# An attention and MLP kernel on one core: hand-placed order against a list scheduler, with new loads, hash moves and relus

## The chip, the cores and the metric

The kernel runs on one core of a Trainium2 chip. The metric is device time in microseconds (us), as the median of several executions. Before the change it was 365.38 us (3 runs, 363.77 to 365.77). TensorE does matmuls, VectorE and ScalarE work on elements, GpSimd also works on elements, and SyncE ("sync") mostly issues DMAs. The profiles count the DMA queues of all issuing engines on the same 16 DMA engines. "PSUM" is the memory that matmuls write to.

A run is called slow when it is over 1.5% above the fastest run of the same kernel.

## The reference

```python
# q, k, v: (4, 8, 768, 64); proj: (64, 6); w_ch1: (512, 2048); w_ch2: (2048, 512)
q_bits = (np.einsum('bhsd,dk->bhsk', q, proj) > 0)
k_bits = (np.einsum('bhsd,dk->bhsk', k, proj) > 0)
mask = q_bucket[:, :, :, None] == k_bucket[:, :, None, :]   # all six bits equal
scores = np.where(mask, scale * np.matmul(q, k.transpose(0, 1, 3, 2)), -1e9)
attn = softmax(scores)                     # (shortened here)
x = np.matmul(attn, v)                     # heads side by side: (4, 768, 512)
xn = (x - mu) / np.sqrt(var + 1e-06) * g_ln
out = x + np.maximum(xn @ w_ch1, 0.0) @ w_ch2
```

The mask is computed as more score: a matmul over the six hash bits adds a large value for each equal bit, and a bias in the exp takes the total away again.

## The kernel before

The work is 72 steps (batch, 256 queries, 4 heads, 256 keys): scores on TensorE, exp on ScalarE, and attention times v ("av") on TensorE. Every six steps finish a unit of 256 tokens. A unit is normalized on VectorE and turned by two transposing DMAs into the tile `xnT`. Then come 8 chunks of ff1 with a relu each, and 8 chunks of ff2. Chunks of unit u are placed between the steps of later units. Each function has a key, and the keys, set by hand, decide the order.

```python
def load_x(b, g, t):                       # q or k of the next batch, a whole tile
    nc.sync.dma_start(out=X[b, g, t], in_=qk_view((q, k)[t], b, g))
def hash_move(b, g, c, i):                 # 16 for each group: bits of 6 partitions to their place
    nc.sync.dma_start(out=G[b, g][32*i : 32*i+NB, :, W*c : W*c+W],
                      in_=Bt[b, g][32*c + 8*i : 32*c + 8*i + NB])
def flip(u):
    for qt in range(2):
        nc.sync.dma_start_transpose(out=xnT[u][:, qt], in_=xc[u][:, qt])
def ff1(u, p, bank):
    ...                                    # 8 matmuls that read xnT[u]
    nc.vector.tensor_scalar_max(hb[u][:, 2*p : 2*p+2], f1, 0.0)
...
at(S0 - 10, load_x, b, g, 0)               # S0: the first step that needs the group
at(6 * u + 6.12, flip, u)
```

Loads, moves, transposes and stores go through one queue, sync's; only w2 (GpSimd) and small constants (ScalarE) take another.

The softmax here doesn't subtract the row's maximum and nothing guards it: scores larger than these inputs give would overflow.

## Time and profile before

| | before |
|---|---|
| span of the profiled run | 363.9 us |
| TensorE busy | 312.7 us (86%) |
| first ff1 starts | 65.0 us |
| from there to the end | 298.9 us |
| ff1 waits for relus / for `xnT` | 13.8 / 2.3 us |

The chain of waits shows what a transposed tile takes from issue to landing (start, duration, what):

```profile
113.38 2.44 DMA xnT<-xc
189.57 2.50 DMA xnT<-xc
266.80 2.43 DMA xnT<-xc
```

### The profile page before, as it was taken

What the parts mean: (1) busy time and instruction counts of PE and PEld (TensorE: products, weight loads), DVE (VectorE), ACT (ScalarE), POOL (GpSimd) and SP (SyncE); (2) the same over time, 40 slices, a digit from 0 to 9 for tenths busy, and PEclk for the clock granted to TensorE, in tenths of its full rate; (3) what the DMA queues carried; (4) which work ended last, traced back from release to release, by engine and by line L of the source; (5) the groups of instructions that cost most, each with busy time, mean ns of one, the idle gap of its engine ahead of it and who ended that gap; (6) DMA issues with size and microseconds to landing.
All of it is one profiled execution on the core that took longest, in us unless ns stands there. A gap on an engine that the chain in (4) does not pass through costs nothing.

```text
span 363.9 us, 9678 instructions
## 1 busy us (share of the span) xinstructions
PE 312.7 (86%) x4281; PEld 209.8 (58%) x4344; DVE 183.3 (50%) x373; ACT 144.7 (40%) x76; POOL 100.5 (28%) x106
## 2 busy tenths in 40 slices
PE   8674457989988989989989989898889899897993
PEld 3353335766665666756656657666656567565561
DVE  1427245385662363578444534955624545446341
ACT  2344204662453554445246445533535455442000
POOL 1656142019940010069710010399200100101000
PEclk9989555899999999999999999999999999999899
DMA  7799931991021039860030279700210302203022
GB/s 170 174 243 212 306 112 29 273 260 23 9 64 34 3 88 278 193 141 7 12 78 13 59 204 242 192 7 8 64 35 2 88 2 59 31 2 78 10 59 58
DMA packets 34873, 35.68 MB, mean 98 GB/s; under 512 B 17424, under 2 KB 29712, under 8 KB 34832
## 3 DMA queue, kind: packets, MB, share of 16 engines
q1 hardware_dynamic: 31872, 32.96, 36.0%
q0 software_dynamic: 2112, 2.10, 3.6%
q8 instruction: 34, 0.56, 0.6%
q10 hardware_dynamic: 848, 0.01, 0.2%
q14 instruction: 7, 0.06, 0.1%
HBM read 27.27 MB, written 6.29 MB: 92 GB/s over the span
## 4 chain that ended last, share of the span: by engine, by line
PE 66%; DVE 15%; SPq 5%; DMA 4%; issue 3%; ACT 3%; POOL 1%; ACTq 0%; DVEq 0%; POOLq 0%
PE f L248 19%; PE f L258 18%; PE sc L182 11%; PE acc L206 8%; PE hf L301 4%; SPq L133 4%; DVE hb L252 3%; ACT E L189 3%; PE hp L123 2%; DVE xc L231 2%; DMA w1f<-in_moe_w_ch_dram 2%; DMA xnT<-xc 2%; PE warm L354 2%; DVE x L221 2%; DVE st L223 1%
## 5 line engine op out<-in xcount | busy, mean ns | idle before, releaser
L189 ACT ACTIVATE E<-sc,bias_sb 128x2048 bf16<-128x2048 f32 x72 | 141.6, 1967 | 173.9 <-PE sc L182 173.9
L248 PE MATMUL f<-xnT,w_sb 128*128 128x256 bf16 x768 | 99.7, 274 | 16.3 <-DVE hb L252 13.8
L248 PEld LDWEIGHTS <-w_sb 128*128 128x128 bf16 x768 | 72.4, 98 | 39.1 <-issue 23.0
L252 DVE TENSOR_SCALAR hb<-f 128x512 bf16<-128x512 f32 x96 | 65.6, 683 | 52.7 <-PE f L248 51.4
L258 PE MATMUL f<-w_sb,hb 128*128 128x512 bf16 x321 | 86.9, 385 | 3.5
L232 POOL TENSOR_SCALAR rs<-mv 128x2 f32<-128x2 f32 x12 | 6.1, 512 | 199.6 <-DVE mv L230 199.6
L182 PE MATMUL sc<-qb,kb 32*128 32x256 bf16 x1152 | 54.2, 275 | 0.0
L258 PEld LDWEIGHTS <-hb 128*128 128x128 bf16 x384 | 35.2, 99 | 30.5 <-issue 3.2
L206 PEld LDWEIGHTS <-E 128*128 128x128 bf16 x1152 | 43.1, 100 | 11.4 <-issue 10.5
L206 PE MATMUL acc<-vaug,E 128*128 128x65 bf16 x1152 | 49.5, 198 | 0.0
L265 DVE SCALAR_TENSOR_TENSOR res<-f,rs,x 128x512 f32<-128x512 f32 x24 | 18.0, 751 | 54.7 <-PE f L258 50.7
L182 PE MATMUL sc<-G 6*128 6x256 bf16 x576 | 41.9, 280 | 4.0 <-ACT E L189 3.9
L97 POOL TENSOR_SCALAR qb<-T 128x1536 bf16<-128x1536 f32 (+1 forms) x10 | 30.6, 3059 | 13.4 <-DVE T L288 13.4
L182 PEld LDWEIGHTS <-G 6*128 6x128 bf16 x576 | 15.4, 92 | 29.7 <-issue 28.6
L182 PEld LDWEIGHTS <-kb 32*128 32x128 bf16 x1152 | 30.8, 96 | 2.0
L301 PE MATMUL hf<-T,pfull 128*128 128x256 f32 x48 | 18.1, 514 | 13.6 <-DVE T L288 13.5
L83 DVE STREAM_TRANSPOSE T<-X 128x384 f32<-128x384 f32 x48 | 25.4, 555 | 0.0
L301 PEld LDWEIGHTS hf<-T,pfull 128*128 128x128 f32 x48 | 10.7, 246 | 18.7 <-DVE T L288 17.2
L223 DVE BATCH_NORM_STATS2 st<-x 128x6 f32<-128x256 f32 x48 | 18.1, 418 | 0.8
L221 DVE TENSOR_TENSOR x<-acc,rc 128x512 f32<-128x512 f32 x24 | 16.6, 692 | 0.8
L86 DVE TENSOR_SCALAR G<-hf 128x256 bf16<-128x256 f32 x12 | 5.1, 425 | 23.5 <-PE hf L301 23.5
L219 DVE RECIPROCAL rc<-acc 128x8 f32<-128x8 f32 x24 | 4.9, 205 | 21.1 <-PE acc L206 21.1
(35 smaller groups left out, 147.9 us busy)
## 6 DMA issues: line engine op xcount, KB each, us to landing
vnat<-in_v_dram SPq DMA_DIRECT2D x32, 192.0 KB
out_dram<-res SPq DMA_DIRECT2D x48, 128.0 KB
X<-in_q_dram SPq DMA_DIRECT2D x6, 768.0 KB
X<-in_k_dram SPq DMA_DIRECT2D x6, 768.0 KB
w1f<-in_moe_w_ch_dram SPq DMA_DIRECT2D x4, 1024.0 KB
w_sb<-in_moe_w_ch_dram POOLq DMA_DIRECT2D x4, 512.0 KB, 8.5
X<-in_q_dram SPq DMA_DIRECT2D x6, 256.0 KB
X<-in_k_dram SPq DMA_DIRECT2D x6, 256.0 KB
```

What stands on the lines that cost most here:

```text
L83: nc.vector.transpose(d[:, j, kj0 : kj0 + n], s[:, j, kj0 : kj0 + n])
L97: eng.tensor_scalar(qb[b, g][:, :, lo:hi], src, QS, None, op0=AOP.mult)
L182: nc.tensor.matmul(sc[s][:, i, 256 * kk : 256 * kk + 256], lh, rh, start=(rep == 0), stop=(rep == 2), skip_group_check=True,)
L189: nc.scalar.activation(E[s], sc[s], AF.Exp, scale=EXP_SCALE, bias=bias_sb)
L206: nc.tensor.matmul(acc[u, g][:, qt, (D + 1) * i : (D + 1) * (i + 1)], E[s][:, i, 256 * kk + P * qt : 256 * kk + P * qt + P], vaug[u // 3][ ...
L221: nc.vector.tensor_tensor(xo, a[:, :, :, 0:D], rc.to_broadcast([P, 2, 4, D]), op=AOP.mult)
L223: nc.vector.bn_stats(stats[u][:, qt, g], xt[u][:, qt, 256 * g : 256 * g + 256])
L248: nc.tensor.matmul(f1[:, n].rearrange("p (t x) -> p t x", t=2), w1_sb[:, dt, P * nt : P * nt + P], xnT[u][:, :, dt], start=(dt == 0), stop ...
L252: nc.vector.tensor_scalar_max(hb[u][:, 2 * p : 2 * p + 2], f1, 0.0)
L258: nc.tensor.matmul(f2[u, t], hb[u][:, nt, P * t : P * t + P], w2_sb[:, nt], start=(nt == 0), stop=(nt == NNT - 1),)
L265: nc.vector.scalar_tensor_tensor(res[u][:, t], f2[u, t], rstd[u][:, t : t + 1], xt[u][:, t], op0=AOP.mult, op1=AOP.add,)
L301: nc.tensor.matmul(hp[:, :256], pfull[:, j], tp[:, j], start=(j == 0), stop=(j == 1))
```

## The change

A scheduler replaces the hand-set order. Each piece of work becomes a task with an engine, an assumed duration and a key, and a plan is computed before the program is written. Several other parts come with it. Cut to its core, with cuts marked by "...":

```diff
-        nc.sync.dma_start(out=X[b, g, t], in_=qk_view((q, k)[t], b, g))
+                load_x(b, g, t, (0, 3), "aq", S0 - 11 + 0.5 * t, S0 - 11)   # "aq": ScalarE's queue
...
-        for c in range(CC):                      # v in four pieces of 32 partitions
-            nc.sync.dma_start(out=vnat[b][32 * c : 32 * c + 32, hs : hs + 4], ...)
+        src = v[b].rearrange("h (w kj) d -> w h (kj d)", kj=KJ)             # 128 partitions at once
+        load_v(b, 0, 4, "aq", S0 - 9, S0 - 10)
...
+    # tails of batch 0's queries: small hash group and 16 moves each, on sync
+        hash_group(0, g, ((0, 256, 128),), "f1", 3.0 + 3 * g)
+                task("sp", 420, key + 0.1 * (4 * c + i), mv, ..., dma=4600)  # one move: 420 ns assumed
...
-        nc.vector.tensor_scalar_max(hb[u][:, 2 * p : 2 * p + 2], f1, 0.0)
+        task(("dve", "act"), (620, 620), key - 50, relu, ...)               # whichever is free first
...
-        nc.sync.dma_start(out=w1f[n], ...)       # then casts on VectorE
+        task("pq", 1500, key, lambda e: e.dma_start(out=w1_sb[...], in_=w1ap[...]))   # casting DMA
...
+    for s in range(NS):
+        step(s, s < 9, s)                        # first nine steps in head halves
...
+    order = plan()
+        for t in order:
+            t.fn(ENG[t.by])
```

Its intent: start the MLP earlier, take relus off VectorE's path, and let no engine wait for an order that was set by hand.

## The prediction

> **What bounds the kernel now.** I read the busy tenths in 40 slices first, because a mean over the whole span mixes stages.
>
> ```profile
> PE   8674457989988989989989989898889899897993
> PEclk9989555899999999999999999999999999999899
> DMA  7799931991021039860030279700210302203022
> ```
>
> One slice is 9.1 us. TensorE is nearly full from the eighth slice (64 us) to the end; before that it is half empty, and in three slices its granted clock is halved. So there are three stages: a head of about 65 us, a dense stretch, a short tail. The table of stretches agrees: from 70 to 330 us TensorE is busy 240 of 260 us, and that count is low, since the ff2 group has 321 of its 384 matmuls on record (63 x 0.216 us = 13.6 us missing). From 0 to 70 us it is busy 47 us, part of it at half clock.
>
> Next, the timeline of TensorE in the head:
>
> ```profile
> 38.61 0.40 PE L182 MATMUL sc<-G 6*128 6x256 bf16 x4
> ...
> 46.85 2.08 PE L301 MATMUL hf<-T,pfull 128*128 128x256 f32 x4 [5.78 <-DVE T L288]
> 50.19 2.08 PE L301 MATMUL hf<-T,pfull 128*128 128x256 f32 x4 [1.26 <-DVE T L288]
> 53.53 2.08 PE L301 MATMUL hf<-T,pfull 128*128 128x256 f32 x4 [1.26 <-DVE T L288]
> 55.54 0.40 PE L182 MATMUL sc<-G 6*128 6x256 bf16 x4
> ...
> 65.00 1.89 PE L248 MATMUL f<-xnT,w_sb 128*128 128x256 bf16 x8
> ```
>
> Step 5 is scored at 38.6 us, step 6 only at 55.5, behind four late query pieces. They share two-deep buffers, so each is loaded, transposed, hashed and cast before the next, and the load of w1 with its VectorE casts stands among them. The first ff1 starts at 65.0 us, and 363.9 - 65.0 = 298.9 us follow. In the waits of the dense stretch (66 to 330 us) the losses on TensorE are few:
>
> ```profile
> PE f L248 <- DVE hb L252: 11.8, 10, 1.2
> PE hp L123 <- DVE hb L252: 2.4, 3, 0.8
> PE f L248 <- DMA xnT<-xc: 2.3, 2, 1.3
> PE sc L182 <- ACT E L189: 0.7, 1, 0.7
> ```
>
> (Total us, times, longest.) A relu on VectorE that frees its PSUM bank late costs 14.2 us; the rest is small. So the kernel is bound by TensorE's order and work after 65 us, and by arrival of data before.
>
> Two more views bear on the change: the instructions of the hash tile, and the DMA counters for 66 to 69 and 69 to 72 us.
>
> ```profile
> L133 SPq DMA_DIRECT2D G<-B x96: 720/721/961, 87.0 to 271.2; - x96
> DMA packets 278, 1.19 MB, mean 397 GB/s; under 512 B 30, under 2 KB 102, under 8 KB 278
> DMA packets 462, 0.64 MB, mean 213 GB/s; under 512 B 53, under 2 KB 460, under 8 KB 462
> ```
>
> Each small move of hash bits holds the sync queue 0.72 us (in the queue's timeline 7 take 5.36 us, so 0.77 apart). The first counter is mainly whole q and k tiles over 128 partitions; the second is v in pieces of 32 partitions. Both stretches have the DMA engines full.
>
> **What the Trainium skill says.** "SBUF — State Buffer", section "Door 1: The DMA port swizzle", says that bandwidth follows the number of SBUF ports reached, and that partitions 0..31 reach 8 of 16. The trace agrees: 213 against 397 GB/s, though packet sizes differ too. "TensorE: Matmul & The Clock Gate", Part 1, says that the clock is half after an idle window of about 3.4 us. The trace agrees: the same hash piece takes 1.13 us early and 2.08 us from 36 to 55 us. "DMA: Bandwidth & Descriptors", section "SWDGE vs HWDGE vs iDMA", says a cast during DMA must be issued from GpSimd; before already does so for w2 (0.74 to 1.01 us of GpSimd each, 7.1 to 10.4 us to landing). "ScalarE: Activation LUTs", section "What ACT_TABLE_LOAD costs", gives 280 ns + 0.833 ns per element with a pointer bias, 186 ns without, 93 ns overlapping between neighbours. The trace agrees: 2048 columns take 1967 ns.
>
> **The change, part by part.** I also read the order of instructions of the built changed kernel, with its waits; no time is in it.
>
> *Work.* TensorE keeps its 72 steps, 96 ff1 and 96 ff2 chunks. First hashes by full tile fall from 12 to 8 (4 x 1.1 us), two small hash groups come in (about 0.6 us each), 14 warm matmuls go. Steps 0 to 8 scored by head halves lose half of the four-row packing, 9 x 0.77 = 7 us more, but in the head, where TensorE waits anyway. ScalarE: 144 exps of 1024 columns by the formula (280 + 853 - 93 = 1.04 us) are 150 us against 141.6, plus 54 of 96 relus at 0.61 to 0.70 us, 35 us: 185 of about 340 us. VectorE loses 54 x 0.683 = 36.9 us of relus and 9.1 us of w1 casts, and gains some 10 us: 96 transposes of about 0.42 us for 34.5 us in all, a slower xc, bit scalings. GpSimd loses the multiplying q casts: 6 x (4.10 - 1.47) + 4 x (1.49 - 0.62) = 19 us. None of these three is a bound, so none of it counts by itself.
>
> *Head.* All of batch 0 is now queued at once on the sync queue, v over 128 partitions: 4.7 MB. Of it 0.8 MB are 512-byte packets, which ran at 266 GB/s (4 to 6 us): 3.0 us. The whole k tile, 0.8 MB at 397: 2.0 us. The other 3.1 MB, in 1 to 1.5 KB packets, I put at 330 GB/s: 9.5 us. From 2 us this ends at 16.5 us alone. The casting DMAs stand on GpSimd behind the first v cast (1.47 us) and add (1.81 us), so from about 13 us they take about half of the engines, and the last q piece lands near 21 us. VectorE transposes both q tails (four of 0.42 us after the last landing) before it can evict the hash of group 0: its bits are ready near 24 us. (Before, the last first hash was evicted at 55.6.)
>
> Then comes what I think the plan underrates. The sync queue issues 32 small moves, 16 for each group, and behind them the two transposes of the first normalized tile. 32 x 0.77 = 24.5 us, so the moves end near 48.5; two transposes of 1.2 us and 2.4 us to land (the chain shows 2.44) give a first ff1 at about 53 us. The plan's constant for a move is 0.42 us. Also the built order takes the semaphores of hardware-queue DMAs from eight in turn, shared by sync and ScalarE: ScalarE's first prefetch for batch 1 must wait for a move of group 1, and the exps of steps 7 and 8 stand behind such loads. By the same spacing that holds them to 44 and 47 us, still inside the 53.
>
> So ff1 starts 12 us earlier, with step 9's scores (0.77 us), one more AV (0.5) and fall (0.2) already done: 13.5 us. A slow clock at that point should cost as before (its first ff1 took 1.70 us in the chain), so it cancels.
>
> *Dense stretch.* Of the waits for relus (14.2 us, plus 2.1 in the tail) I credit 10: two engines share them, and the order puts other chunks between, but some will stand behind an exp pair of 2.1 us. Loads moved to ScalarE and whole-tile stores free queue time nothing waits for: 0. The unit of about 25 us stays otherwise.
>
> *Tail.* Before, the last eight stores start after both halves; from the last result (359.1) to the end are 4.8 us. After, one 256 KB store is left: one issue of 0.4 and a landing of about 2 us, 2 us saved. The gap before the last unit's ff1 (2.05 us, then ff2 at half clock, 4.2 us for 12 matmuls) stays in kind: 24 ff2 matmuls, 5.2 us, must cover a normalization, two transposes and their landing, about 7.6 us. 0.
>
> *Sum.* 363.9 - 13.5 - 10 - 2 = 338.4 us span; times run about 1.6 us over the span (365.4 against 363.9): 340 us.
>
> **Rivals.** (A) Head fully mended: if a move costs near the plan's 0.42 us (these move 6 partitions of one piece, not of two), 32 take 13.4 us, ff1 starts at 42 us, and the time is 329. For it: the plan's other constants match the trace (ff1 870 against 0.87, transposing DMA 1250 against 1210). Against: 720 was the minimum of 96. (B) The planned order doesn't fit the chip: relus behind exps, transposes behind moves, each unit losing 1 us or so again; the 10 us are given back: 350. For it: queues are in order, and a plan from fixed durations knows no lateness; against: VectorE and ScalarE have slack and catch up whenever TensorE waits. (C) ScalarE as bound: 2.1 us of exps and 0.5 of relu in a step of 4.1 us say no; it would need its waits for DMA semaphores to recur in every batch, 355. (D) Only the head's transfers mattered: then the head's gain is nearer 16 us and the relus give 3: 343.
>
> **Range and chances.** The head is uncertain by some 5 us each way (landing of q, move cost), the dense stretch by 6, the tail by 2; together about 8, and I widen it for a new stall: 328 to 351. For "within 2%" it would have to stay above 358, with no gain in the dense stretch and half of the head's lost: 3 in 100.
>
> **What would show it.** First ff1 at 49 to 57 us, with sync's moves back to back before it and the wait named as the transposed tile; step 0 scored by about 10 us instead of 13.6; v near 330 GB/s; waits of ff1 for relus at 6 us or less in the dense stretch, on both engines; the last store under 3 us after the last result. Wrong would be: ff1 before 45 us (moves cheaper), or TensorE's waits past 60 us above 20 us in all (the plan misfits), or a clock that stays halved beyond 60 us.

## More of the kernel before

The timeline of sync from 58 to 68 us (start, duration, engine, line, operation, tiles, count) says:

```profile
60.48 2.60 SPq L238 DMA_TRANSPOSE xnT<-xc  x2
63.13 0.57 SPq L101 DMA_DIRECT2D X<-in_q_dram  x1
63.75 0.43 SPq L101 DMA_DIRECT2D X<-in_k_dram  x1
64.22 3.89 SPq L145 DMA_DIRECT2D vnat<-in_v_dram  x7
```

The two transposes leave first, and the loads of the next batch follow in the same queue.

## The result, and the profile after

The changed kernel took 377.51 us (median of 4 runs, 375.76 to 381.15), the kernel before 364.71 us in the same rounds. Ratios here are the mean time of one kernel's fast runs over that of the other's of the same rounds, so not quite the ratio of the medians quoted. This ratio is 1.036 (95% interval 1.028 to 1.045). It is slower by 3.6%; 340 us had been predicted.

The same slices as in the prediction, now of the kernel after (one slice is 9.5 us):

```profile
PE   5997751799995994999995995999995999999995
PEclk9999555699998999699998999899996999999999
DMA  7999259202101139501101139401101102011011
```

TensorE has a deep hole in the sixth to eighth slices (47 to 76 us). It also has five single slices of 4 or 5 tenths in the dense stretch, and the granted clock dips in many of them. Its waits (total us, times, longest):

```profile
PE f L445 <- DMA xnT<-xc: 32.9, 9, 10.3
PE sc L348 <- ACT E L361: 7.2, 5, 4.1
PE sc L348 <- DMA G<-Bt: 2.6, 1, 2.6
```

No wait of ff1 for a relu is left (before: 13.8 us), and a wait for the transposed tile has taken its place: 32.9 us, before 2.3. The chain of waits of the kernel after shows three kinds of lateness; these are the start and end of the head, and two tiles of the dense stretch:

```profile
53.28 1.36 SPq L428
54.74 13.65 DMA xnT<-xc
68.44 3.57 PE f L445 x16
...
116.80 1.23 SPq L428
118.13 2.34 DMA xnT<-xc
...
142.09 1.32 SPq L428
143.50 8.07 DMA xnT<-xc
```

The tile at 116.80 lands as fast as ever, but its transposes leave late. VectorE had its input ready at 112.1 us, and sync was then in the middle of small moves (timeline of sync, 100 to 120 us):

```profile
106.24 10.44 SPq L280 DMA_DIRECT2D G<-Bt  x13
116.80 2.53 SPq L428 DMA_TRANSPOSE xnT<-xc  x2
```

13 moves in 10.44 us are 0.80 us each; the plan assumed 0.42. The same happens at 202.4 and 285.5 us, behind 15 moves each time, and each time the transposes leave 4.7 to 4.9 us after their input is ready. The tile at 142 us leaves at once, but takes 8.07 us to land instead of 2.3; another at 227.5 us takes 7.10. In the head both come together: input ready at 45.96, issue at 53.28 behind 32 moves, landing only 13.65 us later. ScalarE's timeline from 47 to 58 us shows what left at the same time:

```profile
53.36 0.95 ACTq L290 DMA_DIRECT2D vnat<-in_v_dram  x2
56.93 0.35 ACTq L199 DMA_DIRECT2D X<-in_q_dram  x1
57.37 0.47 ACTq L199 DMA_DIRECT2D X<-in_k_dram  x1
```

And the DMA queues in the stretch 58 to 63 us (q10 is ScalarE's queue, q1 sync's; packets, MB, share of the time of 16 engines):

```profile
q10 hardware_dynamic: 663, 1.04, 94.0%
q1 hardware_dynamic: 757, 0.19, 22.8%
```

While the two transposes move their 0.26 MB over some 15 us, the loads on the other queue move megabytes.

### The profile page after: what moved, and what is told of

Its sections match the earlier page's. It is cut to its first block, busy times and chain, and to the rows that moved or that the text cites.

```text
span 379.4 us, 9868 instructions
## 1 busy us (share of the span) xinstructions
PE 326.0 (86%) x4346; PEld 215.1 (57%) x4346; DVE 160.1 (42%) x335; ACT 187.3 (49%) x201; POOL 89.3 (24%) x111
## 4 chain that ended last, share of the span: by engine, by line
PE 60%; SPq 15%; DMA 15%; DVE 5%; issue 3%; ACTq 0%; ACT 0%; DVEq 0%
PE f L445 23%; PE f L466 12%; DMA xnT<-xc 12%; PE sc L348 11%; SPq L280 8%; PE acc L371 7%; SPq L283 4%; PE hf L237 3%; SPq L428 3%; PE hp L258 2%; DMA G<-Bt 2%; DMA pfull<-in_proj_dram 1%; PE acc L379 1%; DVE xc L424 1%; DVE st L415 1%
## 5 line engine op out<-in xcount | busy, mean ns | idle before, releaser
L361 ACT ACTIVATE E<-sc,bias_sb 128x1024 bf16<-128x1024 f32 x144 | 152.9, 1111 | 117.1 <-PE sc L348 108.5
L445 PE MATMUL f<-xnT,w_sb 128*128 128x256 bf16 x768 | 102.6, 284 | 32.9 <-DMA xnT<-xc 32.9
L466 PE MATMUL f<-w_sb,hb 128*128 128x512 bf16 x384 | 97.7, 386 | 1.7 <-DVE res L474 1.7
L455 DVE TENSOR_SCALAR hb<-f 128x512 bf16<-128x512 f32 x42 | 29.0, 690 | 110.2 <-PE f L445 96.4
L348 PE MATMUL sc<-qb,kb 32*128 32x256 bf16 x1152 | 62.9, 286 | 0.0
L453 ACT ACTIVATE hb<-f 128x512 bf16<-128x512 f32 x54 | 32.2, 597 | 61.7 <-PE f L445 61.7
L348 PE MATMUL sc<-G 6*128 6x256 bf16 x576 | 50.3, 289 | 9.9 <-ACT E L361 7.2
L371 PEld LDWEIGHTS <-E 128*128 128x128 bf16 x1152 | 43.5, 101 | 14.4 <-issue 9.6
L209 DVE STREAM_TRANSPOSE T<-X 128x256 f32<-128x256 f32 x96 | 48.3, 625 | 4.7 <-DMA X<-in_q_dram 2.4
L348 PEld LDWEIGHTS <-kb 32*128 32x128 bf16 x1152 | 36.0, 99 | 3.7 <-issue 0.3
L224 POOL CAST qb<-T 128x1536 bf16<-128x1536 f32 (+1 forms) x10 | 11.2, 1130 | 53.8 <-DVE T L209 46.7
L424 DVE SCALAR_TENSOR_TENSOR xc<-x,mv,g_bc 128x512 bf16<-128x512 f32 x24 | 17.7, 763 | 0.1
L237 PE MATMUL hf<-T,pfull 128*128 128x256 f32 x32 | 13.6, 584 | 3.2 <-DMA pfull<-in_proj_dram 2.5
```

Of the source, the lines that this page charges most:

```text
L209: e.transpose(d[:, j, kj0 : kj0 + n], s[:, j, kj0 : kj0 + n])
L237: e.matmul(tiles[hn][:, :256], pfull[:, j], tiles[tn][:, j, sl], start=(j == 0), stop=(j == 1))
L348: e.matmul(tiles[sn[i // 2]][:, i % 2, 256 * kk : 256 * kk + 256], lh, rh, start=(rep == 0), stop=(rep == 2), skip_group_check=True,)
L361: task("act", 1040, key + 0.001 * x, lambda e, x=x: e.activation(tiles[en[x]], tiles[sn[x]], AF.Exp, scale=SCALE, bias=bias_sb), r=[(sn[x] ...
L371: e.matmul(a[:, qt, D1 * i : D1 * i + D1], tiles[en[x]][:, i % 2, 256 * kk + P * qt : 256 * kk + P * qt + P], tiles["vaug", b][:, 4 * g + ...
L424: task("dve", 600, key, lambda e, qt=qt: e.scalar_tensor_tensor(tiles[cn][:, qt], tiles[xn][:, qt], tiles[mn][:, qt, 0:1], g_bc, op0=AOP.s ...
```

## The experiments

Two theories stood at the start. Theory 1: the prefetch loads, moved to ScalarE's queue and one step earlier, run beside the transposes and slow them. Theory 2: the transposes stand behind the small moves in sync's queue. The rival to both was that ScalarE, with exps and relus, or something else had become slower. Edits of who issues a DMA keep the planned order; edits of full tails, late loads, relus and whole steps change the input of the planner, which then orders everything anew, so their worth includes that. In the names, "tails" means full query tails in the head, "pool" the moves on GpSimd, and "late" loads at a later moment; "tpl" is all three, and "tps" is tails, pool, and loads on sync.

### Loads later, same queue (late_loads)

```diff
-                load_x(b, g, t, (0, 3), "aq", S0 - 11 + 0.5 * t, S0 - 11)
+                load_x(b, g, t, (0, 3), "aq", S0 - 11 + 2.5 + 0.5 * t, S0 - 11 + 2.5)
-        load_v(b, 0, 4, "aq", S0 - 9, S0 - 10)      # and the second half likewise
+        load_v(b, 0, 4, "aq", S0 - 9 + 1.5, S0 - 10 + 1.5)
```

> The changed kernel with only the loads of batches 1 to 3 planned later (q and k by 2.5 steps, v by 1.5), still on ScalarE's queue; each batch's loads then leave after the two transposes of the normalized tile instead of beside them. Theory 1 (the transposes land late because loads on the other queue share the DMA engines with them): the landing of the first transposed tile falls from 13.7 us to under 4 us, first ff1 near 58 instead of 68.4 us; the landings of 8.1 and 7.1 us in the dense stretch fall to 2.3; all waits of ff1 for the transposed tile fall from 32.9 to 15 us or less; time 377.5 - 10 - 7 = 360 us. Theory 2 (the transposes are late because they stand behind 6-partition moves on sync): no part of the moves is changed, so the waits stay near 33 us and the time near 377. Theory 3 (the kernel is longer for other reasons, such as ScalarE's two shares of work): 377.

Measured: ratio to before 0.984 (0.981 to 0.987), median 364.92 us of 21 runs on two levels, 358.1 to 362.6 (8 fast ones) and 364.1 to 368.4 (13 slow ones). Its profile is of a slow run. The head's tile landed in 2.29 us, and ff1 started at 58.5 us. The chain still has landings of 4.38 and 3.88 us, and 20.7 us of waits remain where 15 were expected. Theory 1 holds, and it is not all.

### Moves of batches 1 to 3 on GpSimd (late_moves_to_pool)

```diff
-            t.fn(ENG[t.by])
+            t.fn(nc.gpsimd if t.dma == 4600 and t.key > 9 else ENG[t.by])
```

Only the issuer changes; the planned order of every other engine is kept.

> The changed kernel with the moves of hash bits of batches 1 to 3 issued by GpSimd instead of sync, every other engine's order kept; the 32 moves of the head stay. Theory 2: three waits of 3.8 to 4.9 us in the dense stretch belong to transposes issued 10 us late behind 13 to 15 moves; they vanish, and with the clock dips behind them the time falls by 10 to 12 us, to 366. Theory 1: only the waits beside loads (138 to 145 and 224 to 230 us, about 9 us together) would matter and these stay: 375 or more. The head's first ff1 stays near 68 us for both.

Measured: 355.63 us, ratio 0.966 (0.958 to 0.975). Its waits on TensorE:

```profile
PE f L445 <- DMA xnT<-xc: 14.4, 5, 8.2
PE sc L348 <- ACT E L361: 7.1, 5, 4.0
```

Theory 2 holds, at twice the size that I gave it. I had counted three stalls of about 4 us. The waits fell by 32.9 - 14.4 = 18.5 us, and TensorE's busy time by 326.0 - 318.6 = 7.4 us, most likely because fewer matmuls ran at a reduced clock (the mean granted clock after the first ff1 was 0.98, in the changed kernel 0.95); the spans differ by 24.3. (This profile is of a run classed slow.) A move on GpSimd took 0.567 us on average against 0.72 on sync.

### No moves in the head (full_tails)

```diff
-                if t == 1 or kp == 0:
-                    first_hash(0, g, t, kp, ...)
-        hash_group(0, g, ((0, 256, 128),), "f1", 3.0 + 3 * g)
+                first_hash(0, g, t, kp, ...)
```

> The changed kernel with the query tails of batch 0 hashed in full columns (as for the other pieces) instead of by the small group with 32 moves; everything else by the same planner. Theory 2: the transposes are issued as soon as the normalized tile is ready, near 46 us, instead of behind the moves at 53.3, so first ff1 comes 6 to 8 us earlier, near 61, time 370. Theory 1: the loads of batch 1 no longer wait for semaphores of the moves and start just as early, so the landing stays long (8 us or more) and ff1 starts at 57 to 62. Neither: time 377 and steps 6 to 8 no earlier than 38 to 50 us.

Measured: 370.25 us, ratio 1.011 (1.003 to 1.020), unclear against before. The transposes left at 43.15 us instead of 53.28, but landed 14.70 us after issue, and ff1 started at 59.5. So 10 us at issue brought 9 at ff1 and 7 at the end. Both theories said numbers like these: leaving earlier helps, and the landing stays long.

### All three together (tails_pool_late)

> All three together: full query tails in the head, moves of batches 1 to 3 on GpSimd, loads planned later. If theories 1 and 2 together are the whole loss, all waits of ff1 for the transposed tile fall from 32.9 us to under 6, ff1 starts before 54 us, and the time is 377.5 - 14 (head) - 20 (dense) = 343 us, faster than the kernel before (364.7). If something else lengthens the dense stretch (ScalarE's exps and relus, VectorE's slower transposes) it stays above 355 with the waits of ff1 for that in the trace.

Measured: 332.92 us, ratio 0.908 (0.901 to 0.916). Waits for the transposed tile were 3.2 us, and ff1 started at 46.1 us. The expectation was 10 us too careful, because the moves are worth more than I had counted. The rival falls: ScalarE's exps have the same mean, 1111 ns, in this run and in the changed kernel, and TensorE waits 2.1 us for them.

### What each part is worth beside the others

Two more corners complete the table. `tails_late` is all three without the GpSimd moves, `pool_late` all three without the full tails. The third, all three without the late loads, is `tails_pool`, told below.

> Full query tails and late loads, moves of batches 1 to 3 still on sync. Beside the run of all three (332.9) this is the worth of the moves in the dense stretch. From late_moves_to_pool alone (377.5 to 355.6) it is 22 us: 355. If much of those 22 us came from clearing sync's queue for loads' semaphores, less: 343 to 350. The late issues behind 13 to 15 moves (three, 4 us each with the clock dips) would give at least 345.

Measured: 348.90 us. TensorE's waits for the tile were 13.6 us, in five waits.

> Late loads and GpSimd's moves, but the head's 32 moves for the query tails stay. Beside the run of all three (332.9) this is the worth of the head's moves once the rest is mended: first ff1 near 58 us (as with late loads alone) instead of 46, so 12 us: 345. If the planner's other work fills that gap: under 337.

Measured: 345.88 us, ff1 at 57.5 us, as expected. `tails_late` did not come out at 355, as if the moves were worth their 22 us again, but in the range given for a smaller share (343 to 350): beside the other two repairs they are worth 16 us. Whether the rest came from semaphores, as that expectation supposes, was not tested. The ratios to before:

| mended | ratio |
|---|---|
| nothing (the changed kernel) | 1.036 |
| tails | 1.011 |
| late loads | 0.984 |
| moves on GpSimd | 0.966 |
| tails, late loads | 0.951 |
| late loads, GpSimd | 0.946 |
| tails, GpSimd (second time) | 0.955 |
| all three | 0.908 |

Taking one away from the last line costs 3.8% (tails), 4.3% (moves) or 4.7% (loads): 14, 16 and 17 us of 365. All three are needed, and none contains another.

### Queue or moment? (tails_pool, tails_pool_sync, tails_pool_timed)

`tails_pool` leaves the loads at their early moment on ScalarE's queue. `tails_pool_sync` has the same planned order, but sync issues them:

```diff
-            t.fn(nc.gpsimd if t.dma == 4600 and t.key > 9 else ENG[t.by])
+            t.fn(nc.gpsimd if t.dma == 4600 and t.key > 9 else nc.sync if t.by == "aq" and t.key > 0 else ENG[t.by])
```

> Full query tails and moves of batches 1 to 3 on GpSimd, as in the run of all three, but the loads at the changed kernel's own times (beside the transposes, on ScalarE's queue). If the loads beside the transposes cost what the run with late loads alone suggests (12 us), this is near 345 us, with a first landing of 10 us or more in the head; if the two earlier repairs had already made the landings harmless, 334.

Measured: 349.19 us, but only one of four runs was fast (341.89), so there is no ratio. The first tile landed in 13.06 us.

> The same kernel and the same order of every other engine, but the loads of batches 1 to 3 issued by sync, as the kernel before did, in front of the transposes where the plan has them there. Theory 1a (a second queue that shares the engines is the fault): transposes on the same queue as the loads land sooner, and the time falls towards 335. Theory 1b (the bytes in flight are the fault, whichever queue they are on): the transposes now stand behind whole loads of 0.8 to 1.6 MB, landing 8 to 14 us as before or later, and the time is 345 to 352.

Measured: 331.56 us, ratio 0.908 (0.903 to 0.913). On sync no exps stand ahead of the loads, and the first q and k tiles left before 22 us instead of at 38 and 40 us. Queue and moment had both changed. So in `tails_pool_timed` ScalarE writes one column of the tile where its load stood, and sync's load must wait for that:

```diff
+    def mark(e, b, tile_):
+        if not b:
+            return e
+        nc.scalar.copy(tile_[:, 0, 0:1], bias_sb)
+        return nc.sync
-        ... lambda e: e.dma_start(out=tiles[name][:, :, cols], in_=src[:, :, cols]),
+        ... lambda e: mark(e, b, tiles[name][:, :, cols]).dma_start(out=..., in_=...),
```

> As the run with full tails and GpSimd's moves (349.2), but each load of batches 1 to 3 is issued by sync after ScalarE has written one column of its tile at the load's old place in ScalarE's order: same moments to within about 1 us, other queue. If the second queue is the fault: in the head the first transpose lands behind 1.6 MB of loads issued 3 to 4 us before it, the second behind 0.8 MB more, first ff1 near 50 us instead of 57, time 336 to 341. If the moment is the fault, not the queue: first ff1 at 56 us or later, time 346 to 351.

Measured: 337.26 us, ratio 0.920 (0.912 to 0.927). Since `tails_pool` had one fast run only, both ran again on one chip.

> The same kernel as tails_pool. If its fast runs are near 342 and slow ones near 349, the queue costs 342 against tails_pool_timed's fast 333 to 338, some 6 us; if fast runs are near 349, some 12 us. First landing in the head 10 us or more in a fast run too, if the second queue is the fault whatever the state.

> The same kernel as tails_pool_timed. Loads on sync's queue at ScalarE's moments: fast runs 333 to 338 again, first landing 7 to 8 us (the transposes wait for the loads ahead of them), under 6 us in the dense stretch. If it is not below tails_pool_again's fast runs by over 1 per cent, the queue is not the fault.

Measured: ratios 0.955 (0.950 to 0.960) with loads on ScalarE's queue and 0.925 (0.921 to 0.929) with the same loads on sync's. The fast runs lie at 347.2 to 350.0 and 336.6 to 340.4 us. The level of `tails_pool`'s one fast run, 341.89, did not come back; measured by it, all later runs of this kernel would be slow. Still, all ten runs with two queues (341.89 to 356.86) lie above all ten with one (333.10 to 340.38); fastest against fastest is 8.8 us. Two tiles that landed beside loads, in the chain of the run with two queues (a slow run, 352.1 us of span; the earlier profile, slow too, has 13.06 and 5.00):

```profile
44.79 12.78 DMA xnT<-xc
...
127.77 9.41 DMA xnT<-xc
```

And of the run with one queue (a fast run):

```profile
44.24 8.01 DMA xnT<-xc
...
122.67 4.86 DMA xnT<-xc
```

No fast run of this kernel with two queues was profiled; fast runs of the changed kernel and of full_tails, with the same two queues, show landings of 13.65 and 14.70. The moments are the same to about 2 us, not exactly: the first v load leaves 0.7 us before the first transpose with two queues, and 1.4 us after it with one. My reading: in one queue the transposes only wait for the loads ahead of them, and those have all the engines; in two queues they also share with loads that left after them. So queue and moment both matter. At nearly the same moments the second queue costs 3% (9 to 11 us). At a later moment the second queue is as good (0.908, tails_pool_late) as sync's queue with loads that leave early (0.908, tails_pool_sync).

### Smaller load packets (tails_pool_512)

`X` and v tiles of batches 1 to 3 get a column of padding after every 128 columns, so that each load is cut into pieces of 512 bytes. To fit one DMA, v is read in another order, so the result is wrong. To make room, the 10 warming matmuls of 512 columns became 13 of 384 (4.34 us instead of 4.45).

```diff
-        new = [sb(name, [P, CC, KJ * D], F32, "X", 4)] if kp[0] == 0 else []
+        new = [sb(name, [P, CC, 387], F32, "X", 4)] if kp[0] == 0 else []      # 3 x (128 + 1)
+        ... out=tile.rearrange("p c (a y) -> p c a y", y=129)[:, :, :, 0:128] ...
```

> The run with full tails and GpSimd's moves but early loads on ScalarE's queue, its order of instructions unchanged; only the loads of batches 1 to 3 are cut into 512-byte pieces (tiles with one column of padding after every 128; v of these batches is read in another order, so the result is wrong on purpose, the bytes are the same). Theory 1c (the DMA engines take packets of the two queues in turn): two transposes are about 1100 packets of 256 bytes, some 69 for each engine, and each stands behind one load packet of 0.12 to 0.19 us; 69 x (0.025 + 0.12 to 0.19) = 10 to 15 us, which fits the 13.1 us seen. With load packets of about 0.03 to 0.05 us it is 69 x 0.06 to 0.08 = 4 to 5 us: landing in the head 4 to 6 us, waits of ff1 for the transposed tile 19 -> 7 us or less, time 349 -> 337 to 341. Theory 1d (bytes share the engines, whatever the packets): landing stays near 13 us, time 349.

Measured: 349.37 us, ratio 0.956 (0.952 to 0.961). The head's tile landed in 8.45 us, but two tiles of the dense stretch took 10.71 and 8.26, and the waits were 20.2 us. One thing besides the size of the pieces changed: in the head, the issue of one of these loads took 0.55 to 4.15 us on ScalarE's queue, instead of 0.33 to 0.41. Theory 1c falls in the form in which I put it. From 46 to 54 us the queues moved, first with large pieces (`tails_pool_again`), then with small ones:

```profile
q10 hardware_dynamic: 989, 1.60, 100.6%
q1 hardware_dynamic: 1051, 0.25, 19.9%
```

```profile
q10 hardware_dynamic: 2500, 1.27, 87.5%
q1 hardware_dynamic: 1088, 0.26, 34.3%
```

With large pieces one transposing packet went for about one load packet (1051 to 989) over these 8 us, but not within them: from 50 to 52 us it was 101 to 322, from 52 to 54 us 415 to 141. With small pieces it was 2.3 load packets to one (2500 to 1088). These counts show no packets in turn. How the engines share two queues stays open.

### Relus on VectorE alone (tpl_relu_dve, best_relu_dve)

```diff
-        task(("dve", "act"), (620, 620), key - 50, relu, ...)
+        task("dve", 620, key - 50, relu, ...)
```

> All three repairs, with the relus on VectorE alone as in the kernel before (the planner orders anew). My prediction's step: two engines for the relu save 10 us of waits of TensorE in the dense stretch; then this run is near 343 us with 8 to 14 us of ff1 waiting for VectorE's relu. Rival: the waits of before came from its fixed order, and a planner that knows VectorE's load places chunks around it; then it stays within 3 us of 333.

Measured: 333.01 us, ratio 0.908 (0.897 to 0.918), against 332.92 and 0.908 with two engines. The rival is right: the relus' second engine is worth nothing here.

> The best kernel (no halves, full tails, moves on GpSimd, loads on sync: 328.5) with relus on VectorE alone. On the run of all three this changed nothing (333.0 against 332.9). My credit says 338; the rival says 328.5 within 3 us.

Measured, on the best kernel: 329.97 us, ratio 0.903 (0.899 to 0.908), against 328.48 and 0.900. The intervals overlap.

### More warming matmuls (tpl_warm24, tps_warm24)

```diff
-        for _ in range(NWARM):     # 10
+        for _ in range(24):
```

> All three repairs, with 24 warming matmuls instead of 10 (the number of the kernel before), the order otherwise the same. If the half clock from 8.6 to 20 us is what the idle 2.4 us after the tenth warming matmul cost, the first hash pieces take 1.0 to 1.1 us again instead of 2.1, step 0 is scored near 12 us instead of 13.8 and step 1 near 14.5 instead of 17.6; of that at most 3 us reach the end: 330 to 332. If the arrival of batch 0 sets the head anyway: 333, unchanged.

> Best kernel so far with 24 warming matmuls instead of 10, order the same. On the run of all three the same edit gave 332.2 against 332.9, unclear. If the half clock of 8.6 to 20 us reaches the end: 328 to 330; if not, 331.6.

Measured: 332.16 us (ratio 0.902, 0.895 to 0.909) against 332.92 on the kernel with late loads: not told apart. On the kernel with loads on sync, 333.78 us (0.915, 0.911 to 0.919) against 331.56: no gain, if anything a loss. There the first four hash pieces ran at full clock again (1.13 us for one, instead of 2.08), but a wait of 4.2 us for VectorE came later, and the clock was halved behind that.

### Whole steps in the head (tps_no_halves)

```diff
-        step(s, s < 9, s)
+        step(s, False, s)
```

> Best kernel so far (full tails, moves on GpSimd, loads on sync: 331.6) with the first nine steps scored by all four heads at once instead of in halves. My prediction charged halves 7 us of TensorE time in the head that it waits anyway; if that is right the time stays within 2 us. If the head has become TensorE-bound, it gains 4 to 7 us: 325 to 328. If halves matter for ScalarE's start, it loses 2 or more.

Measured: 328.48 us (328.21 to 328.63), ratio 0.900 (0.897 to 0.903), against 331.56 with halves. Halves cost 3 us once the head is mended (the two intervals, 0.897 to 0.903 and 0.903 to 0.913, just touch). This version beats both kernels: 10% faster than before. Its clock in 40 slices:

```profile
PEclk9589959999999999999999999999999999999999
```

And the wait that this study is about, from the same run's waits:

```profile
PE f L445 <- DMA xnT<-xc: 1.5, 3, 0.8
```

From the seventh slice (49 us) to the end the clock is full. First ff1 is at 46.1 us, and 280.3 us follow.

One thing could not be tried: giving the planner the true time of a move. With 760 ns instead of 420 it finds no order at all and stops at its own assertion before a program is written, so no such kernel ran.

## Why the prediction was wrong

**The step that failed** is this sentence: "Loads moved to ScalarE and whole-tile stores free queue time nothing waits for: 0." The loads did more than leave sync's queue. They went to a second queue, at a moment when the transposes are issued; with the other two delays repaired, this queue costs 9 to 11 us (tails_pool_again against tails_pool_timed_again). With it falls the "2.4 us to land" in the head, which I took from a kernel whose loads stood behind the transposes in the same queue. It was 13.65. The late loads alone bring it back to 2.29. The prediction had the moment in hand: it held the exps behind ScalarE's first loads to 44 and 47 us (48.4 and 53.1 in the trace) and put the transposes at 48.5 (53.3), but asked only what waits behind those loads, not what runs beside them.

A second step failed, and it weighs more: "The unit of about 25 us stays otherwise." It charges the 96 moves of the dense stretch nothing. The transposes left 4.7 to 4.9 us late behind them three times, and taking these moves off sync's queue was worth 14 to 26 us, depending on what else was mended.

**The head.** Predicted first ff1 at about 53 us, measured 68.4, 15.1 us more than my terms add up to (48.5 + 2.4 + 2.4 = 53.3). The moves were right: 32 x 0.77 predicted, 23.45 us measured for 32. The bits they wait for came at 29.7 us instead of 24, so the moves ended 4.8 us late. The landing took 11.2 us more, and the issue counted 1 us less. Step 0 was scored at 15.1 us, not 10. TensorE waited 2.5 us for the projection columns, then hashed at half clock, and the chain that ended last runs through these hashes until 29.9 us. In the mended kernels more warming gained nothing; in the changed kernel, whose moves wait for such a hash, it was not tried.

**The dense stretch.** My sum left 298.9 - 10 - 2 - 1.5 = 285.4 us after the first ff1; 311.0 were measured, 25.6 more. Of these, 32.9 - 10.3 - 2.3 = 20.3 us are waits for the transposed tile. Against them stand 6.2 us of relu waits that vanished beyond my credit of 10 (13.8 for ff1 and 2.4 for the hash group before, none listed after). The rest is 25.6 - 20.3 + 6.2 = 11.5 us. I put most of it down to clock: the mean granted clock after the first ff1 was 0.95 against 0.99 before, and an ff1 matmul took 284 ns on average against 274. TensorE's busy time there was 281.5 us; in the best kernel, with nearly the same work, it was 272.0 at 0.99 (in tails_pool_timed_again, with the same 3882 matmuls, 271.8). That is 9.5 us, and this share is read from profiles, not isolated by a run.

**The relus.** Right in kind and more than right in size: all of the waits vanished. The reason that I gave was wrong. Two engines did not do it, since VectorE alone gives the same time. Nor did a freer VectorE: with all relus it was busy 61% of the span in tpl_relu_dve, 50% before. The order, in which other chunks stand between an ff1 and the next use of its bank, is the remaining reading; the runs show only what does not do it.

**The tail.** Predicted 2 us saved. Before, 4.8 us passed from the last result to the end; after, the last result is done at 376.2 us and the span ends at 379.4, 3.2 us. 1.6 us saved: right.

**Halves.** "... in the head, where TensorE waits anyway": in the mended kernel, where the head waits less, they cost 3 us of the 7 charged. In the changed kernel itself this was not run.

**The rivals.** B named the right failure, "transposes behind moves", and priced it at 1 us a unit and 350 us in all, too little. I argued against B that VectorE and ScalarE have slack; the engine without slack was sync, whose order I had read and whose 0.72 us a move I had quoted. I applied it to the 32 moves of the head, where nobody could miss it, and not to the 96 of the dense stretch, where the plan assumes 0.42. A fell (32 moves took 23.45 us, not 13.4), and so did D, since the head gained nothing. C (ScalarE as bound) was rightly refused: ScalarE was busy 187.3 us (185 predicted), and of the 7.2 us that TensorE waited for its exps, 1.2 came after the first ff1. What I listed as proof of error, "TensorE's waits past 60 us above 20 us in all", is what the profile showed.

**Where the expected gain went.** It was there: 32 us below before once three things are repaired, and 37 in the best version (loads on sync, whole steps). In the changed kernel two delays of one small tile, the wait in sync's queue and the sharing of the DMA engines, ate it and 13 us more. The granted clock dips in the slices of these stalls, so the work behind them was slower too.

## What to carry to other kernels

A small DMA that TensorE waits for should share neither its queue with a row of tiny moves ahead of it nor its moments with bulk loads on another queue; ask of every prefetch what is in flight beside it, not only whether its own data is early enough. A plan made from assumed durations is only as good as the worst of them, so check each constant of the scheduler against the trace at every place where it is used. When one part of a change removes a wait, undo that part alone before giving it the credit.

## What the Trainium skill lacked or had wrong

- "DMA: Bandwidth & Descriptors", section "Issuing engines are not separate DMA queues", says that issuing from several engines "will only save the time on the sequencer", and that the transfers interleave. It does not say that this can cost. Here the same loads at nearly the same moments cost 3% (348.7 against 337.8 us, means of fast runs) on ScalarE's queue instead of sync's; that a waiting transpose shares the engines with loads that left after it is my reading.
- The same page, section "Queues, rings and completion order", says that a DMA engine takes packets of its queues in turn, each packet of several descriptors. The counts here cannot test that: a packet of a transpose, as the profile counts it, is one piece of about 240 bytes (0.26 MB in 1088). What a transposing DMA loses beside another queue's loads is not given: 2.3 us to land became up to 14.70.
- I found on no page what the issue of a tiny DMA costs in time on this chip ("DMA: Bandwidth & Descriptors" only counts sequencer cycles for earlier generations, in its part on trn3 B0): 6 partitions took 0.66 us (one piece) or 0.72 us (two) on sync, and 0.57 us on GpSimd.
- I found on no page what a VectorE transpose of 128x256 costs when its destination is strided: 624 ns (median of 96), against 414 (median of 24) before. The order of the destination is the difference that I see; no run changes it alone. The prediction had counted 0.42 us for one.
